# Splitting the first four operands of the second layer's y products during the last pair of h

## The chip, the cores and the metric

The kernel runs on one core of a Trainium2 chip. The metric is the device time in microseconds (us) of one execution; the times of several executions are compared by their median. The profiles are single executions recorded by the hardware profiler.

## What is computed

Chunked attention over 4 x 768 tokens feeds two feed-forward layers, each with an inner width of 2048 and an outer width of 512, in float32:

```python
def _moe_ref(x, w_in, w_out):
    h = x @ w_in
    g = h - np.tanh(h)
    return g @ w_out

def _moe2_ref(x, w_in, w_out, alpha):
    h = x @ w_in
    g = np.maximum(h, 0.0) + alpha * np.minimum(h, 0.0)
    return g @ w_out

def reference(...):
    attn_out = _attn_ref(**attn_kwargs)
    x = attn_out.transpose(0, 2, 1, 3).reshape(B * S, H * D)
    x = _moe_ref(x=x, **moe_kwargs)
    return _moe2_ref(x=x, **moe2_kwargs)
```

x has 3072 rows of 512, w_in is 512 x 2048 and w_out 2048 x 512.

## The kernel before

**Numbers in two parts.** Every float32 matrix that TensorE (PE) multiplies is split into a high part in fp32r and the rest (split_f32, and prep for the second layer's y): ScalarE (ACT) copies to fp32r, then VectorE (DVE) or GpSimd (POOL) subtracts. A product is three matmuls: high by high, high by rest, rest by high (PASS).

**Stages.** Attention and the first layer run together, in six blocks of 512 tokens (emit_h, emit_g, emit_y, evac_y). evac_y copies a finished block's four y tiles out of PSUM, two by ACT and two by DVE, and stores them to DRAM (y1d). In the sixth block the copies use a tag of their own, "zy" with two buffers. The second layer then runs in three blocks of 1024 tokens (the loop over b at L866). Each has an h stage and a y stage, and both save multiplications with Strassen's seven products (Winograd's variant) on 2 x 2 blocks.

**The h stage.** pair_h runs eight times in a block, for p = 0 to 7. It makes seven products of 6 matmuls (L404), in the source's order m = 1, 6, 5, 7, 2, 3, 4, and combines them in PSUM: hs is a copy of product 1 (ACT), hu adds product 6 (DVE), product 5 is added to hu (DVE, L421; called the d5 add here), hv is a copy of that (ACT, L446), and products 3 and 4 are accumulated on what the adds and copies leave. So product 3 waits for hv. prelu makes each of the four results of a pair: two ACT operations (L412, L413) and one DVE operation (L414), into gx or gy. Two POOL subtractions follow (L455 and L456).

**The y stage.** Its left operands are made from gx, gy and t3 by prep (L467 to L482), for s = 0 to 55, eight for each of the products in ORDER = (1, 6, 5, 2, 7, 3, 4). One prep is an ACT copy into go (L477) and a subtraction into go's second half (L479, the split), on DVE for most and on POOL for s = 2 to 7 and some later ones. For product 6 (s = 8 to 15) DVE first adds into a PSUM bank (L474) and afterwards updates gx (L481). y_product (L498) is 6 matmuls on one operand: the two with the high part first, or three for each of two banks. prep runs LEAD = 6 operands ahead in the source.

**What sets the order.** The Tile framework's scheduler orders each engine's instructions when the program is built. issue_after(ins) puts the instructions of a block that run on the engine of ins behind ins on that engine. On the chip each engine takes its instructions in that order. Tiles are given by pools; w has 34 buffers of 4 KB, which hold gx, gy, the operands of h and y, and half of the weights that load_in brings.

In the source all preps stand behind the last pair_h of a block:

```python
            for s in range(LEAD):
                prep(b, s)
            for s in range(7 * P2):
                if s + LEAD < 7 * P2:
                    prep(b, s + LEAD)
```

Of the kernel before, what the change touches and what calls it, by code (L numbers as in the profile page):

```python
# [7 lines left out]
FP32 = mybir.dt.float32  # L8
# [29 lines left out]
def chunk_attention_two_ffn_kernel(  # L38
# [12 lines left out]
    nc = tc.nc  # L51
# [10 lines left out]
    blocks1 = BLOCKS1  # L62
# [3 lines left out]
    def f32(ap):  # L66
        return ap.bitcast(FP32)

    const = ctx.enter_context(tc.tile_pool(name="const", bufs=1))
    w_p = ctx.enter_context(tc.tile_pool(name="w", bufs=2 * NF + 2))  # L70
# [17 lines left out]
    stage = {}  # L88
# [174 lines left out]
    last = {}  # L263
# [59 lines left out]

    def evac_y(l, b, n, t0):
        ys = yp.pop((l, b))
        for j, y in enumerate(ys):
            if l == 0 and b == len(blocks1) - 1:
                s = stage["z"].tile([128, 512], FP32, tag="zy", name="ys", bufs=2)
            else:
                s = t_p.tile([128, 512], FP32, tag="t", name="ys")  # L330
            dst = y1d[b, :, j, :] if l == 0 else out[(t0 + j) * 128:(t0 + j + 1) * 128, :]
            if j % 2 == 0:
                nc.scalar.activation(out=s, in_=y, func=ACTF.Copy)
            else:
                nc.vector.tensor_copy(out=s, in_=y)
            nc.scalar.dma_start(out=dst, in_=s)
# [5 lines left out]
    P2 = NF // 2  # L342
    NB = NTILE // 8
    NO = 7 * P2 // 2
    LEAD = 6
    wo2 = {}
    win = {}
    xop = {}
# [6 lines left out]
    def load_out(i):  # L355
        mi, pp = divmod(i % NO, P2 // 2)
        w = zr.tile([128, 2, 2, 256], FP32R, tag="wo", name="wo")
        nc.sync.dma_start(out=f32(w).rearrange("k p a n -> k (p a n)"), in_=w2o[ORDER[mi]][pp])
        wo2[i] = w

    def load_in(i, q):
        p = i % P2
        n = 2 if q < 3 else 1
        pool, tag = (w_p, "w") if i % 2 == 0 else (stage["z"], "z")
        w = pool.tile([128, 2, n, 256], FP32R, tag=tag, name="wi2")
        nc.sync.dma_start(
            out=f32(w).rearrange("p a s n -> p (a s n)"),
            in_=w2i[p][:, 1024 * q:1024 * q + 512 * n])
        win[i, q] = w
# [22 lines left out]
    def x2_work(b):  # L392
        return ([lambda w=w: load_x2(b, w) for w in (12, 11, 22, 21)]
                + [lambda m=m: sum_x2(b, m) for m in (5, 6, 7, 4)]
                + [lambda m=m: split_x2(b, m) for m in (1, 6, 5, 7, 2, 3, 4)])
# [14 lines left out]
    def prelu(t, h, f):  # L410
        n = t_p.tile([128, 512], FP32, tag="t", name="n")
        nc.scalar.activation(out=n, in_=h, func=ACTF.Relu, scale=-1.0)  # L412
        nc.scalar.activation(out=n, in_=n, func=ACTF.Copy, scale=alpha_neg[:, f:f + 1])  # L413
        nc.vector.scalar_tensor_tensor(  # L414
            out=t, in0=h, scalar=0.0, in1=n, op0=ALU.max, op1=ALU.add
        )

    def pair_h(i):
        b, p = divmod(i, P2)
# [40 lines left out]
    def y_bank(b, m):  # L460
        if (b % 2 == 0) == (m in (1, 6)):
            return ps_y.tile([128, 512], FP32, tag="y", name="yb")
        if m in (1, 5):
            return ps_h.tile([128, 512], FP32, tag="h", name="yb")
        return ps_h2.tile([128, 512], FP32, tag="h2", name="yb")

    def prep(b, s):  # L467
        mi, p = divmod(s, P2)
        m = ORDER[mi]
        x, y, d3 = gx[b, p], gy[b, p], t3[b, p // 2][:, p % 2]  # L470
        op = w_p.tile([128, 2, 512], FP32R, tag="w", name="go")
        if m == 6:
            src = y_bank(b, 7)
            nc.vector.tensor_tensor(out=src, in0=d3, in1=x[:, 0], op=ALU.add)  # L474
        else:
            src = {1: x[:, 0], 5: y[:, 0], 2: y[:, 1], 7: d3, 3: x[:, 1], 4: x[:, 0]}[m]
        nc.scalar.activation(out=op[:, 0], in_=src, func=ACTF.Copy)  # L477
        eng = nc.gpsimd if (m == 1 and p > 1) or (m not in (1, 6) and p % 4 == 3) else nc.vector
        eng.tensor_tensor(out=op[:, 1], in0=src, in1=f32(op[:, 0]), op=ALU.subtract)  # L479
        if m == 6:  # L480
            nc.vector.tensor_tensor(out=x[:, 0], in0=y[:, 1], in1=src, op=ALU.subtract)  # L481
        gop[b, s] = op  # L482
# [4 lines left out]
    def y_product(b, s, tiles=(0, 1)):  # L487
        mi, p = divmod(s, P2)
        m = ORDER[mi]
        into = {2: 1, 3: 5, 4: 7}.get(m, m)  # L490
        if m == into and p == 0 and 0 in tiles:
            yd[b, m] = [y_bank(b, m) for _ in range(2)]
        w = wo2[b * NO + mi * (P2 // 2) + p // 2][:, p % 2]
        w = w.rearrange("k a (i n) -> k a i n", i=2)
        op = gop[b, s]
        for i in tiles:
            for n, (a, c) in enumerate(PASS):
                nc.tensor.matmul(  # L498
                    out=yd[b, into][i], lhsT=w[:, a, i], rhs=op[:, c],
                    start=(m == into and p == 0 and n == 0), stop=(p == P2 - 1 and n == 2),  # L500
                    skip_group_check=True,
                )

    def y_done(b, m, tiles=(0, 1)):
        add = lambda o, p, q: nc.vector.tensor_tensor(out=o, in0=p, in1=q, op=ALU.add)
        if m in (1, 6, 5):
            for i in tiles:
                tag = "gl" if m == 6 else "gh"
                e = ye[b, m, i] = g_p.tile([128, 512], FP32, tag=tag, name="ye")
                d = yd[b, m][i]  # L510
                if m == 6:
                    add(e, d, ye[b, 1, i])
                    continue
                if m == 5:
                    add(d, d, ye[b, 6, i])
                nc.scalar.activation(out=e, in_=d, func=ACTF.Copy)
            return
        into, h, t = {2: (1, 0, 0), 7: (7, 1, 1), 3: (5, 0, 1), 4: (7, 1, 0)}[m]
        if 0 in tiles:
            ye[b, "st"] = w_p.tile([128, 16, 2, 32], FP32, tag="w", name="st")  # L520
        st = ye[b, "st"]
        for i in tiles:
            d = src = yd[b, into][i]
            if m == 7:
                src = t_p.tile([128, 512], FP32, tag="t", name="c")
                add(src, d, ye[b, 5, i])
                add(d, d, ye[b, 6, i])
            nc.vector.transpose(out=st[:, :, i], in_=src.rearrange("k (b n) -> k b n", n=32))
        t0 = 1024 * b + 512 * t
        split = len(tiles) == 1  # L530
        for a in range(4):
            dst = out[t0:t0 + 512, 256 * h + 64 * a:256 * h + 64 * a + 64]
            dst = dst.rearrange("(b i) (e j) -> i b e j", i=32, e=2)
            src = st[32 * a:32 * a + 32]
            if split:
                dst, src = dst[:, :, tiles[0]], src[:, :, tiles[0]]
            (nc.scalar if split and a % 2 else nc.sync).dma_start(out=dst, in_=src)
# [189 lines left out]
    if True:  # L727
# [138 lines left out]
        for b in range(NB):  # L866
            more = b + 1 < NB
            for p in range(P2):
                i = b * P2 + p
                if i > 0:  # L870
                    pair_h(i)
                for q in range(4):
                    win.pop((i, q))
                if p + 2 < P2:
                    for q in range(4):
                        load_in(i + 2, q)
            early, late = [], []
            if more:
                work = x2_work(b + 1)
                early, late = work[:8], work[8:]  # L880
                late[3:3] = [lambda q=q: load_in((b + 1) * P2, q) for q in range(4)]
                late += [lambda q=q: load_in((b + 1) * P2 + 1, q) for q in range(4)]
            for s in range(LEAD):
                prep(b, s)
            for s in range(7 * P2):
                if s + LEAD < 7 * P2:
                    prep(b, s + LEAD)
                if more or s < 6 * P2:
                    y_product(b, s)
                    if s % P2 == P2 - 1:  # L890
                        y_done(b, ORDER[s // P2])
                    i = b * NO + s // 2 + 4
                    if s % 2 and i < NB * NO:
                        load_out(i)
                if s >= 2 * P2 and s % 2 == 0 and early:
                    early.pop(0)()
                if s >= 4 * P2 and late:
                    late.pop(0)()
            if not more:
                for i in range(2):  # L900
                    for p in range(P2):
                        y_product(b, 6 * P2 + p, (i,))
                    y_done(b, 4, (i,))
# [61 lines left out]
```

## Time and profile before

| what | value |
| --- | --- |
| three runs | 1112.11, 1113.10, 1114.18 us; median 1113.1 |
| the profiled execution | 1113.69 us |
| its span, first to last instruction | 1111.9 us |
| PE busy | 1061.2 us, 95% of the span |
| DVE, ACT, POOL busy | 61%, 48%, 41% |
| mean granted TensorE clock | 0.986 of full speed |
| share of the chain that ended last | PE 88%, DVE 3%, DMA 3%, ACT 3%, issue 2%, POOL 1% |
| second layer | from about 616 us to the end |

A row of the timeline gives the start, the duration, the engine, the line, the operation with out<-in, how many instructions are merged, and in brackets the idle time of the engine just before with what ended it. PE matmuls are pipelined: one is drawn as about 0.39 us long, and the next begins 0.227 us after it.

### The profile page before, as it was taken

Reading aid. Unit: us, or ns where it says so; the run is one execution under the profiler, and the core shown is the slowest. Engines: PE = TensorE matmul, PEld = TensorE weight load, DVE = VectorE, ACT = ScalarE, POOL = GpSimd, SP = SyncE. Lnnn points to the kernel's source line nnn. Section 1 sums busy time; section 2 is a strip of 40 time slices with the busy share of each in tenths; the row PEclk is TensorE's granted clock in tenths of the full one; section 3 lists DMA queues with packets and bytes.
Section 4 is the critical chain, followed back from the end, with each engine's and each line's share of the span. In section 5 each row is a group of like instructions: output and inputs, shape, how many; then the busy total and the mean of one; then the engine's idle time right before and its main releaser. Section 6 shows DMA issues by size and latency. Waiting matters only on the chain.

```text
span 1111.9 us, 18216 instructions
## 1 busy us (share of the span) xinstructions
PE 1061.2 (95%) x6912; PEld 866.5 (78%) x6912; DVE 674.1 (61%) x1087; ACT 534.8 (48%) x956; POOL 459.5 (41%) x351
## 2 busy tenths in 40 slices
PE   5699999999999999999999999799998899998998
PEld 4488878888888888888888787688886688876786
DVE  3788765765755675565311355977455966456953
ACT  3566644453544454444332455654465644466540
POOL 3266634444544453444462122546122545122520
PEclk9899999999999999999999999899999899999999
DMA  9673144545564464464420644478835578642476
GB/s 277 259 266 114 58 161 143 199 125 200 182 204 171 145 214 154 156 217 146 134 67 1 220 159 170 147 245 275 242 137 185 166 233 280 209 169 97 152 211 168
DMA packets 99366, 196.22 MB, mean 176 GB/s; under 512 B 36560, under 2 KB 50896, under 8 KB 99280
## 3 DMA queue, kind: packets, MB, share of 16 engines
q1 hardware_dynamic: 93712, 188.52, 51.9%
q10 hardware_dynamic: 5568, 6.56, 1.6%
q8 instruction: 54, 0.88, 0.3%
q14 instruction: 32, 0.26, 0.1%
HBM read 153.10 MB, written 41.94 MB: 175 GB/s over the span
## 4 chain that ended last, share of the span: by engine, by line
PE 88%; DVE 3%; DMA 3%; ACT 3%; issue 2%; POOL 1%; SPq 0%; DVEq 0%; POOLq 0%; ACTq 0%
PE h L274 22%; PE y L313 22%; PE yb L498 20%; PE h L404 18%; PE pv L670 2%; PE sp L586 2%; DMA y1d<-ys 2%; DVE go L479 1%; ACT n L412 1%; DMA qn<-in_q_dram 1%; ACT n L413 1%; PE tp L657 1%; DMA ro<-in_moe_w_out_dram 1%; DVE yb L474 1%; DVE h L421 0%
## 5 line engine op out<-in xcount | busy, mean ns | idle before, releaser
L274 PE MATMUL h<-ring,wt 128*128 128x512 f32 x1152 | 282.2, 392 | 5.8 <-ACT ring L677 2.7
L274 PEld LDWEIGHTS h<-ring,wt 128*128 128x128 f32 x1152 | 216.7, 189 | 52.4 <-ACT ring L677 2.8
L498 PE MATMUL yb<-go,wo 128*128 128x512 f32 x1008 | 237.9, 398 | 16.9 <-DVE go L479 8.5
L498 PEld LDWEIGHTS yb<-go,wo 128*128 128x128 f32 x1008 | 192.6, 192 | 61.8 <-DVE go L479 12.3
L404 PE MATMUL h<-xh,wi 128*128 128x512 f32 x672 | 211.9, 392 | 3.2 <-ACT hs L439 1.2
L299 POOL TENSOR_TENSOR gl<-t,gh 128x512 fp32r<-128x512 f32 x96 | 129.6, 1352 | 173.8 <-ACT gh L298 158.0
L313 PE MATMUL y<-gh,wt 128*128 128x512 f32 x768 | 192.8, 391 | 0.0
L313 PEld LDWEIGHTS y<-gh,wt 128*128 128x128 f32 x768 | 143.1, 188 | 30.5
L290 DVE TENSOR_TENSOR t<-h,t 128x512 f32<-128x512 f32 x96 | 66.0, 687 | 144.6 <-ACT t L289 144.5
L404 PEld LDWEIGHTS h<-xh,wi 128*128 128x128 f32 x672 | 126.1, 188 | 35.1 <-ACT hv L446 5.4
L455 POOL TENSOR_TENSOR t<-gx,gy 128x512 f32<-128x512 f32 x24 | 31.1, 1296 | 200.6 <-DVE gy L414 200.6
L289 ACT ACTIVATE t<-h 128x512 f32<-128x512 f32 x96 | 56.9, 593 | 115.2 <-PE h L274 93.9
L313 PE MATMUL y<-gl,wt 128*128 128x512 f32 x384 | 104.3, 390 | 0.3 <-POOL gl L299 0.3
L298 ACT ACTIVATE gh<-t 128x512 fp32r<-128x512 f32 x96 | 60.5, 630 | 53.0 <-DVE t L290 51.4
L313 PEld LDWEIGHTS y<-gl,wt 128*128 128x128 f32 x384 | 71.9, 188 | 15.7 <-POOL gl L299 0.7
L404 PE MATMUL h<-xl,wi 128*128 128x512 f32 x192 | 74.7, 389 | 0.0
L122 POOL TENSOR_TENSOR ws<-sm,ws 128x512 fp32r<-128x512 f32 x32 | 42.6, 1333 | 57.8 <-ACT ws L121 42.2
L413 ACT ACTIVATE n<-n,alpha_neg 128x512 f32<-128x512 f32 x96 | 66.0, 719 | 0.4
L122 POOL TENSOR_TENSOR wt<-s,wt 128x512 fp32r<-128x512 f32 x32 | 41.3, 1294 | 39.8 <-ACT wt L121 38.1
L404 PE MATMUL h<-x,wi 128*128 128x512 f32 x144 | 56.0, 389 | 0.0
L477 ACT ACTIVATE go<-gx 128x512 fp32r<-128x512 f32 x72 | 41.0, 626 | 27.6 <-PE yb L498 15.9
L479 DVE TENSOR_TENSOR go<-gx,go 128x512 fp32r<-128x512 f32 x42 | 48.7, 1195 | 3.9 <-ACT go L477 3.9
(95 smaller groups left out, 1365.1 us busy)
## 6 DMA issues: line engine op xcount, KB each, us to landing
wo<-w2o SPq DMA_DIRECT2D x84, 512.0 KB, 4.4
wi<-w2i SPq DMA_DIRECT2D x72, 512.0 KB, 4.8
kn<-in_k_dram SPq DMA_DIRECT2D x24, 384.0 KB, 4.5
vn<-in_v_dram SPq DMA_DIRECT2D x24, 384.0 KB, 4.0
ri<-in_moe_w_in_dram SPq DMA_DIRECT2D x16, 512.0 KB, 7.6
ro<-in_moe_w_out_dram SPq DMA_DIRECT2D x16, 512.0 KB, 8.3
pk<-in_moe_w_in_dram SPq DMA_DIRECT2D x16, 512.0 KB, 4.0
pk<-in_moe_w_out_dram SPq DMA_DIRECT2D x16, 512.0 KB, 4.0
```

What stands on the lines that cost most here:

```text
L122: nc.gpsimd.tensor_tensor(out=lo, in0=v, in1=f32(hi), op=ALU.subtract)
L274: last["ffn"] = nc.tensor.matmul(out=h, lhsT=wi[:, a, kk, :], rhs=ring[c][:, s0:s0 + n, kk, :], start=(i == 0), stop=(i == 3 * KD - 1),).ins
L289: nc.scalar.activation(out=t, in_=h, func=ACTF.Tanh)
L290: last["dve"] = nc.vector.tensor_tensor(out=t, in0=h, in1=t, op=ALU.subtract).ins
L298: nc.scalar.activation(out=gh, in_=t, func=ACTF.Copy)
L299: nc.gpsimd.tensor_tensor(out=gl, in0=t, in1=f32(gh), op=ALU.subtract)
L313: mm = nc.tensor.matmul(out=yp[l, b][j][:, :n * 128], lhsT=wo[:, a, j * 128:(j + 1) * 128], rhs=g[c], start=first, stop=final,)
L404: nc.tensor.matmul(out=h, lhsT=w[:, a, 128 * kt:128 * kt + 128], rhs=x[c][:, kt, :], start=(first and j == 0), stop=(j == 5), skip_group_c ...
L413: nc.scalar.activation(out=n, in_=n, func=ACTF.Copy, scale=alpha_neg[:, f:f + 1])
L477: nc.scalar.activation(out=op[:, 0], in_=src, func=ACTF.Copy)
L479: eng.tensor_tensor(out=op[:, 1], in0=src, in1=f32(op[:, 0]), op=ALU.subtract)
L498: nc.tensor.matmul(out=yd[b, into][i], lhsT=w[:, a, i], rhs=op[:, c], start=(m == into and p == 0 and n == 0), stop=(p == P2 - 1 and n == ...
```

## The change

The first EARLY = 4 operands of a block's y stage are prepared ahead of the last pair_h in the source (prep itself is unchanged). The other preps are put behind last["pre"] with issue_after; that is the DVE instruction of the latest prelu, so only their DVE instructions are tied. evac_y's copies of the sixth block of the first layer use two tiles of pool w, each holding two of the four copies, in place of two buffers of tag zy.

```diff
     def evac_y(l, b, n, t0):
         ys = yp.pop((l, b))
+        final = l == 0 and b == len(blocks1) - 1
         for j, y in enumerate(ys):
-            if l == 0 and b == len(blocks1) - 1:
-                s = stage["z"].tile([128, 512], FP32, tag="zy", name="ys", bufs=2)
+            if final:
+                if j % 2 == 0:
+                    pair = w_p.tile([128, 2, 512], FP32, tag="w", name="ys")
+                s = pair[:, j % 2]
...
+    EARLY = 4
...
-        nc.vector.scalar_tensor_tensor(
+        last["pre"] = nc.vector.scalar_tensor_tensor(
             out=t, in0=h, scalar=0.0, in1=n, op0=ALU.max, op1=ALU.add
-        )
+        ).ins
...
             for p in range(P2):
                 i = b * P2 + p
+                if p == P2 - 1:
+                    for s in range(EARLY):
+                        prep(b, s)
                 if i > 0:
                     pair_h(i)
...
-            for s in range(LEAD):
-                prep(b, s)
+            with tc.issue_after(last["pre"]):
+                for s in range(EARLY, LEAD):
+                    prep(b, s)
             for s in range(7 * P2):
                 if s + LEAD < 7 * P2:
-                    prep(b, s + LEAD)
+                    with tc.issue_after(last["pre"]):
+                        prep(b, s + LEAD)
```

Line numbers of the changed kernel are four higher in pair_h and prep (L408 for L404, L425 for L421, L483 for L479, L502 for L498).

**PE at the first block's border between h and y.** The names are the scheduler's: h2 are the PSUM tiles of pair_h (the last pair has four numbers in a row; the third of them holds products 5 and 3, the fourth 7 and 4), yb those of y, go the split operands in the order of s. Before, the last product of h ends and y begins:

```order
L404 MATMUL h2_7021<-xh_6166,wi2_6938 128x512 x2
L404 MATMUL h2_7021<-xl_6167,wi2_6938 128x512
L404 MATMUL h2_7021<-xh_6166,wi2_6938 128x512
L498 MATMUL yb_7112<-go_7091,wo_6482 128x512
L498 MATMUL yb_7113<-go_7091,wo_6482 128x512
```

Now, from the end of product 5 of the last pair through its product 7:

```order
L408 MATMUL h2_7030<-xl_6089,wi2_6932 128x512
L408 MATMUL h2_7030<-xh_6088,wi2_6932 128x512
L502 MATMUL yb_7110<-go_7014,wo_6482 128x512
L502 MATMUL yb_7111<-go_7014,wo_6482 128x512
L408 MATMUL h2_7031<-xh_6092,wi2_6934 128x512
L408 MATMUL h2_7031<-xl_6093,wi2_6934 128x512
L408 MATMUL h2_7031<-xh_6092,wi2_6934 128x512 x2
L408 MATMUL h2_7031<-xl_6093,wi2_6934 128x512
L408 MATMUL h2_7031<-xh_6092,wi2_6934 128x512
L502 MATMUL yb_7110<-go_7014,wo_6482 128x512 x2
L502 MATMUL yb_7111<-go_7014,wo_6482 128x512 x2
L502 MATMUL yb_7110<-go_7017,wo_6482 128x512
```

The first y products stand between products of the last pair. The whole order from product 5 on is: 2 matmuls of s = 0, product 7, 4 of s = 0, 6 of s = 1, 2 of s = 2, product 3, 4 of s = 2, 2 of s = 3, product 4, 4 of s = 3, then s = 4 and on. It is the same at all three borders.

**DVE at the same border.** Before, from the d5 add of the last pair:

```order
L421 TENSOR_TENSOR h2_7020<-h2_7020,hu_7036 128x512
L421 TENSOR_TENSOR gx_7016<-h2_7021,hv_7045 128x512
L421 TENSOR_TENSOR h2_7021<-h2_7021,hu_7036 128x512
L414 SCALAR_TENSOR_TENSOR gx_7016<-gx_7016,n_7055 128x512
L414 SCALAR_TENSOR_TENSOR gx_7016<-h2_7018,n_7065 128x512
L414 SCALAR_TENSOR_TENSOR gy_7017<-h2_7020,n_7075 128x512
L414 SCALAR_TENSOR_TENSOR gy_7017<-h2_7021,n_7087 128x512
L474 TENSOR_TENSOR yb_7132<-t3_6408,gx_6406 128x512
L479 TENSOR_TENSOR go_7091<-gx_6406,go_7091 128x512
L474 TENSOR_TENSOR yb_7144<-t3_6408,gx_6523 128x512
L479 TENSOR_TENSOR go_7094<-gx_6523,go_7094 128x512
```

Now, from the last prelu of pair p = 6:

```order
L418 SCALAR_TENSOR_TENSOR gy_6939<-h2_6944,n_7010 128x512
L483 TENSOR_TENSOR go_7014<-gx_6406,go_7014 128x512
L425 TENSOR_TENSOR hu_7046<-h2_7029,hs_7038 128x512
L483 TENSOR_TENSOR go_7017<-gx_6521,go_7017 128x512
L425 TENSOR_TENSOR h2_7030<-h2_7030,hu_7046 128x512
L425 TENSOR_TENSOR gx_7026<-h2_7031,hv_7055 128x512
L425 TENSOR_TENSOR h2_7031<-h2_7031,hu_7046 128x512
L418 SCALAR_TENSOR_TENSOR gx_7026<-gx_7026,n_7065 128x512
L418 SCALAR_TENSOR_TENSOR gx_7026<-h2_7028,n_7075 128x512
L418 SCALAR_TENSOR_TENSOR gy_7027<-h2_7030,n_7085 128x512
L418 SCALAR_TENSOR_TENSOR gy_7027<-h2_7031,n_7097 128x512
L478 TENSOR_TENSOR yb_7130<-t3_6408,gx_6406 128x512
```

The splits of s = 0 and 1 moved from behind the last prelu to either side of hu. At the second border the first L474 also stood ahead of the d5 add before; now it is behind the last prelu there too.

**ACT at the same border.** Now, from the first pair of L413's of the last pair (n are the prelus' scratch tiles; the early four copies stand right ahead of hv and are not shown):

```order
L417 ACTIVATE n_7075<-n_7075,alpha_neg_79 128x512
L416 ACTIVATE n_7085<-h2_7030 128x512
L417 ACTIVATE n_7085<-n_7085,alpha_neg_79 128x512
L481 ACTIVATE go_7101<-gx_6771 128x512
L481 ACTIVATE go_7104<-gx_6855 128x512
L481 ACTIVATE go_7107<-gx_6938 128x512
L481 ACTIVATE go_7118<-gx_7026 128x512
L416 ACTIVATE n_7097<-h2_7031 128x512
L417 ACTIVATE n_7097<-n_7097,alpha_neg_79 128x512
L481 ACTIVATE go_7129<-yb_7130 128x512
```

Before, all eight copies (s = 0 to 7) stood behind the last prelu's L413. Four of them now stand ahead of hv, and four between the third and the last prelu of the pair. POOL now has, behind pair 6's L456: the splits of s = 2, 3 and 4, the last pair's L455, the splits of s = 5, 6 and 7, and the last pair's L456.

## Rows read from the trace of the kernel before

**Rows 1.** PE, groups by line from 640 us to the end: busy, mean ns, idle before.

```profile
L498 PE MATMUL yb<-go,wo 128*128 128x512 f32 x1008 | 237.9, 398 | 16.9 <-DVE go L479 8.5 <-ACT go L477 8.4
```

**Rows 2.** PE's timeline at the three borders between h and y.

```profile
695.91 0.40 PE L404 MATMUL h<-xh,wi 128*128 128x512 f32 x1
699.12 0.73 PE L498 MATMUL yb<-go,wo 128*128 128x512 f32 x2 [2.80 <-ACT go L477]
702.30 2.93 PE L498 MATMUL yb<-go,wo 128*128 128x512 f32 x6 [2.46 <-DVE go L479]
705.68 6.56 PE L498 MATMUL yb<-go,wo 128*128 128x512 f32 x23 [0.45 <-DVE go L479]
...
856.76 0.50 PE L404 MATMUL h<-xh,wi 128*128 128x512 f32 x1 [1.13 <-ACT hv L446]
...
859.41 0.40 PE L404 MATMUL h<-xh,wi 128*128 128x512 f32 x1
...
869.42 6.84 PE L498 MATMUL yb<-go,wo 128*128 128x512 f32 x24 [0.45 <-DVE go L479]
...
1022.81 0.40 PE L404 MATMUL h<-xh,wi 128*128 128x512 f32 x1
...
1032.57 7.77 PE L498 MATMUL yb<-go,wo 128*128 128x512 f32 x33 [0.45 <-DVE go L479]
```

**Rows 3.** The chain that ended last, y stage of the second block: start, length, matmuls.

```profile
930.21 19.04 PE yb L498 x84
```

**Rows 4.** Windows: us, busy (x) of PE, PEld, DVE, ACT, POOL, then granted clock, DMA.

```profile
628.40:629.50 1.10, 0.00 (x0) 0.00 (x0) 1.07 (x2) 1.08 (x2) 0.00 (x0) 1.00 0.24 93
705.20:707.00 1.80, 1.35 (x4) 1.14 (x4) 1.80 (x4) 0.00 (x0) 1.80 (x2) 0.50 0.00 0
1023.20:1026.00 2.80, 0.01 (x1) 0.00 (x0) 1.99 (x4) 2.80 (x6) 0.36 (x1) 0.90 0.00 0
```

**Rows 5.** ACT's timeline at the third border.

```profile
1015.18 1.33 ACT L413 ACTIVATE n<-n,alpha_neg 128x512 f32<-128x512 f32 x2
1019.50 0.60 ACT L446 ACTIVATE hv<-h 128x512 f32<-128x512 f32 x1 [2.99 <-DVE h L421]
...
1023.63 0.59 ACT L412 ACTIVATE n<-h 128x512 f32<-128x512 f32 x1
1024.11 1.33 ACT L413 ACTIVATE n<-n,alpha_neg 128x512 f32<-128x512 f32 x2
1025.34 4.26 ACT L477 ACTIVATE go<-gx 128x512 fp32r<-128x512 f32 x8
```

**Rows 6.** DVE's timeline: the third border, and three splits at 736.90 with POOL idle.

```profile
736.90 1.89 DVE L479 TENSOR_TENSOR go<-t,go 128x512 fp32r<-128x512 f32 x3
...
1015.93 1.30 DVE L414 SCALAR_TENSOR_TENSOR gy<-h,n 128x512 f32<-128x512 f32 x2 [0.99 <-ACT n L413]
1018.77 0.70 DVE L421 TENSOR_TENSOR h<-h,hu 128x512 f32<-128x512 f32 x1 [0.67 <-PE h L404]
...
1024.87 1.30 DVE L414 SCALAR_TENSOR_TENSOR gy<-h,n 128x512 f32<-128x512 f32 x2 [0.40 <-ACT n L413]
...
1027.39 1.75 DVE L479 TENSOR_TENSOR go<-gx,go 128x512 fp32r<-128x512 f32 x1
...
1032.44 0.68 DVE L479 TENSOR_TENSOR go<-yb,go 128x512 fp32r<-128x512 f32 x1
```

**Rows 7.** POOL's timeline: the third border, and a stretch of the first layer's sixth block.

```profile
562.93 4.77 POOL L122 TENSOR_TENSOR x<-x,xh 128x1024 fp32r<-128x1024 f32 x2
...
1016.70 1.30 POOL L455 TENSOR_TENSOR t<-gx,gy 128x512 f32<-128x512 f32 x1 [7.85 <-DVE gy L414]
1018.08 1.30 POOL L456 TENSOR_TENSOR gy<-gy,gx 128x512 f32<-128x512 f32 x1
```

**Rows 8.** Where the first layer's last y is copied out: ACT, then PE.

```profile
627.78 0.60 ACT L333 ACTIVATE ys<-y 128x512 f32<-128x512 f32 x1 [1.43 <-DMA y1d<-ys]
629.53 0.50 PE L404 MATMUL h<-xh,wi 128*128 128x512 f32 x1 [1.21 <-ACT hs L439]
```

## The prediction

> **What bounds the kernel now.** I read the shares of busy time first: PE is busy for 95% of the span, and the chain that ended last runs through PE for 88%. In the second layer PE therefore sets the time, and a change can win only where PE stands idle or runs slowly. The groups by line come next. From 640 us on, y's matmuls have 16.9 us of idle time ahead of them, all of it in waits for operands, half for ACT's copies and half for the splits [rows 1]. PE's timeline shows where: at each of the three borders between h and y there are three waits, at the first one 2.80, 2.46 and 0.45 us [rows 2].
>
> To price a border I need PE's undisturbed step. In the chain, 84 matmuls take 19.04 us, so 0.227 each [rows 3]. From the start of the last h matmul to the drawn end of the third group of y the borders take 16.33 us (695.91 to 712.24), 16.85 and 17.53, for 1+2+6+23 = 32, 33 and 42 matmuls [rows 2]. At 0.227 each, and 0.16 for the last one's drawn length, that should be 7.4, 7.65 and 9.7. The loss is 8.9, 9.2 and 7.8, together 25.9 us. Only 16.9 of it is idle time; the other 9.0, 3.0 per border, is matmuls at a slow clock: after the waits the window at 705.20 has a granted clock of 0.50, and that at 1023.20 an average of 0.90 [rows 4]. These are the full level of 2.4 GHz and the half of it.
>
> The cause of the waits is on ACT, DVE and POOL at the third border: the eight copies start at 1025.34, behind the last L413 [rows 5], and DVE's first split follows only after the last prelu and an L474 [rows 6].
>
> **The change: what PE gains.** Twenty-four matmuls, those of s = 0 to 3, can fill the border's idle time, and the first of them need nothing of the last pair. I walk through the third border with the times of before.
>
> ACT is done with pair 6 at 1015.18 + 1.33 = 1016.5 [rows 5]. Four copies at 4.26/8 = 0.53 end at 1018.6. That is ahead of hv (1019.50 before), so they cost ACT nothing. s = 0 and 1 are split on DVE, s = 2 and 3 on POOL. POOL is at work from 1016.70 without a break, in L455, L456 and then these splits [rows 7]. So DVE's splits run beside POOL, and I have to choose their price. A split alone takes 1.89/3 = 0.63; one beside POOL took 1.75 [rows 6]; waiting out a whole POOL operation would make it 1.30 + 0.63 = 1.93. I take 1.75, the row with the same operands and the same neighbour. An operation that reads PSUM, like hu and the d5 add, should stay near 0.6: the d5 add took 0.70 with L456 beside it [rows 6, 7].
>
> DVE is free at 1017.23. The split of s = 0 ends at 1019.0, hu (0.6 to the next operation) at 1019.6, the split of s = 1 at 1021.3, the d5 add at 1022.0 instead of 1019.47, and hv at 1022.6 instead of 1020.10. Product 3 waits for hv. But PE, which ends product 5 at about 1018.6 (the d5 add began at 1018.77 behind it), now has 20 matmuls before product 3, product 7 among them: 4.5 us, to 1023.1. So hv's 2.5 us are covered, with 0.5 to spare. Without the cover they would be the fourth wait of a border. Then come 18 matmuls, and product 4 ends at 1027.2 with 20 of the 24 early matmuls done.
>
> **What is left of the waits.** Four more operands (s = 4 to 7) and product 6's eight depend on the last pair still. ACT's copies of s = 4 to 7 begin where the last input of the last prelu stood, 4.0 us behind hv (1025.34 − 1020.10, less 0.59 and 0.66 for the L412 and L413 that now come later) [rows 5]. That is 1026.6, and s = 4 is split on POOL at 1028.5, just as PE wants it. L455 stands between (1.30), and s = 5 comes at 1031.1, while PE is there at 1029.9: a wait of 1.2.
>
> The rest hangs on DVE. The last prelu ended 6.07 us after hv; the four copies put between add 2.13, so it ends at 1022.6 + 8.2 = 1030.8. Everything of product 6 is queued behind it on DVE. Two L474 beside POOL's splits take 3.5 (to 1034.3), four more operations of 0.6 the first two operands (1036.7). Three pairs of operands at 6 x 0.6 = 3.6 follow, and without the last L481 the split of s = 15 is there at 1046.9, with 0.3 for three copies that DVE must wait for at 1047.2. Four matmuls are left then: 1048.1. PE without waits would need 4 + 72 matmuls from 1027.2, so 17.2 us, and end at 1044.4. So 3.7 us remain, wherever they fall. Some six restarts cost about 0.1 each (a matmul behind a wait is drawn 0.50 long, not 0.40 [rows 2]), which makes **4.2 us per border**.
>
> The bounds: if DVE's operations beside POOL took 0.6, hv and the last prelu would come 2.3 earlier and the two L474 2.3 sooner done, and nothing would be late, so 0; at 1.93 each the four of them add 0.7, so 5.0. If the clock fell as before, 3.0 more.
>
> **Other terms.** At the second border PE waited 1.13 for hv in the last pair [rows 2], since an L474 stood ahead of the d5 add there. It no longer does, so 1.1 is gained. Where the first layer's last y is copied out, ACT waits 1.43 for the DMA that stores an earlier tile, and PE then waits 1.21 for hs behind it [rows 8]. Two tiles of pool w for the four copies need no store to end: 1.2 gained. The copies themselves last as long. The tie costs no engine time. Later in y DVE keeps ahead of PE: six matmuls take 1.36 and a split alone 0.63, so tied operands are early enough. Against it stands the first layer's sixth block, where the scheduler's order changed without the source: POOL now has four splits of 4.77/2 = 2.4 us in a row [rows 7], 9.6 us, where at most two stood. I estimate 0.5 lost, between a gain of 1 and a loss of 2.
>
> **The sum.** 25.9 + 1.1 + 1.2 = 28.2 gained, less 3 x 4.2 = 12.6 and 0.5: 15.1 us. The profiled execution took 1113.69, span 1111.9; the median of the runs is 1113.1, 0.6 lower, and I set the forecast on the median: **1098.0 us**.
>
> **The rivals.** *A, the forecast* (60%): 1098, of its own between 1094 and 1102 by the unknown of the sixth block and 1 us per border.
>
> *B, the clock falls again* (16%). The 4.2 us left come as several waits close together. If PE then drops to half speed as it did before, each border pays its 3.0 again: 1101, 1104 or 1107 for one, two or three of them. For it: borders with 16.9/3 = 5.6 us of waits had the fall. Against it: a wait of 1.21 alone left the clock at 1.00 in the window at 628.40 [rows 4], and in the plan no single wait is longer. Beside this, the Trainium skill ("TensorE: Matmul & The Clock Gate", Part 1: The HAM clock gate) says that the clock is set by how busy the array has been recently, so that several small waits can count like a long one. By that rule the price is B's; the fall after the waits before agrees, and the 1.21 us wait neither proves nor denies it.
>
> *C, less contention* (16%). DVE's operations beside POOL cost nearer 0.6, and 0 to 2 us per border are left: 27.7 gained, or 6 less, so 1085 to 1091. For it: POOL's splits and DVE's need not overlap fully. Against it: the 1.75 of the row at 1027.39 [rows 6], the nearest there is.
>
> *D, the early splits hold up h* (4%). If hu, the d5 add and what stands behind are slowed beside POOL as well, product 3 waits for hv, and product 4 and the last prelu behind that. Each such operation costs 1.1 more, and there are seven to the last prelus. It decides from hv later than 1023.1; all seven are 7.7 us per border, less the spare 0.5: 21.6 for three, so about 1120. Against it: the d5 add's 0.70 beside L456 [rows 6, 7].
>
> *E, nothing comes of it* (4%): DVE is the limit through all of product 6 and more, and what PE gains in h it waits for there, 1111 to 1115.
>
> **How the numbers follow.** From A with its margin, most of C and nearly all of B: 1090 to 1106 holds about 8 in 10. About 0.2%, 2.2 us, is what a measurement of this kernel can tell from no change. A, B and C are faster by more than that: 0.92. E gives 0.04 for the same, D 0.04 for slower.
>
> **What would show it.** In the profile of the changed kernel: y's matmuls lie between the last products of h; the idle time ahead of y's matmuls in the second layer falls from 16.9 to about 11, in waits of at most 1.3 us, on POOL's split of s = 5 and DVE's L474; the granted clock stays at 1.00 at the borders; hv ends 2.5 us later with no wait of PE at product 3; the DMA wait of ACT and the wait for hs at 628 us are gone. Wrong would be: a wait ahead of product 3 (D), windows with 0.50 (B), DVE's early splits at 0.6 (C), or an idle time of y still at 16 (E).

## The result and the profile after

| | before | after |
| --- | --- | --- |
| median of four runs, us | 1113.3 | 1094.4 |
| lowest to highest | 1112.11 to 1114.18 | 1093.62 to 1096.97 |
| ratio (95% interval) | 1 | 0.9835 (0.9817 to 0.9854) |
| the profiled execution, its span | 1113.69, 1111.9 | 1096.97, 1094.1 |

The change is 18.9 us faster; 15.1 were forecast. The kernels were run on several chips, so the experiments below go by their ratio to the kernel before on the same chip. "Scaled" means that ratio times 1113.3.

The groups by line from 640 us to the end, PE of the kernel after (the first row answers to [rows 1]):

```profile
L502 PE MATMUL yb<-go,wo 128*128 128x512 f32 x1008 | 235.5, 392 | 5.8 <-DVE go L483 2.7 <-ACT go L481 1.8 <-POOL go L483 1.2
L408 PE MATMUL h<-xh,wi 128*128 128x512 f32 x610 | 192.5, 391 | 0.7 <-DVE gx L418 0.4
```

The idle time ahead of y's matmuls fell from 16.9 to 5.8 us, and no h matmul waits for hv or hs any longer. Where the rest is, PE's timeline of the kernel after shows, the second border first and then the third (answering to [rows 2]):

```profile
856.56 2.88 PE L502 MATMUL yb<-go,wo 128*128 128x512 f32 x12
859.84 4.59 PE L502 MATMUL yb<-go,wo 128*128 128x512 f32 x18 [0.40 <-POOL go L483]
866.08 6.16 PE L502 MATMUL yb<-go,wo 128*128 128x512 f32 x24 [1.65 <-DVE go L483]
873.27 32.10 PE L502 MATMUL yb<-go,wo 128*128 128x512 f32 x140 [1.04 <-DVE go L483]
...
1006.42 0.61 PE L502 MATMUL yb<-go,wo 128*128 128x512 f32 x2
...
1008.24 2.88 PE L502 MATMUL yb<-go,wo 128*128 128x512 f32 x12
1010.96 0.39 PE L408 MATMUL h<-xh,wi 128*128 128x512 f32 x1
...
1014.81 0.39 PE L408 MATMUL h<-xh,wi 128*128 128x512 f32 x1
1015.04 2.88 PE L502 MATMUL yb<-go,wo 128*128 128x512 f32 x12
...
1018.32 9.40 PE L502 MATMUL yb<-go,wo 128*128 128x512 f32 x40 [0.40 <-POOL go L483]
1027.95 3.31 PE L502 MATMUL yb<-go,wo 128*128 128x512 f32 x12 [0.23 <-ACT go L481]
1031.70 57.71 PE L502 MATMUL yb<-go,wo 128*128 128x512 f32 x252 [0.45 <-ACT go L481]
```

The early matmuls lie between the last products of h, and PE has no wait there. Behind h the first border (0.40, 0.23, 0.45 and 0.41 us) and the third have only small waits; the second has 1.65 and 1.04. By the prediction's own method the third border costs, from the last h matmul at 1014.81 to the end at 1089.41, 74.6 us for 317 matmuls, at 0.2267 each and 0.16 for the drawn end: 2.6 us. The first costs 3.2 and the second 4.5 in the same way, 10.3 together, where it was 25.9. Of the 10.3, the waits named here are 5.7; the rest are restarts and gaps too short to be drawn, all at the full clock.

The windows across the second and third border, with the granted clock as the third number from the end:

```profile
1012.00:1024.00 12.00, 11.60 (x52) 9.24 (x51) 8.64 (x12) 6.72 (x12) 8.46 (x6) 1.00 0.41 125
856.00:868.00 12.00, 9.95 (x42) 7.35 (x41) 9.37 (x11) 6.05 (x11) 8.87 (x6) 1.00 0.61 191
```

The clock stays at its full level, 2.4 GHz, where it had been at half [rows 4].

DVE, ACT and POOL of the kernel after at the third border, and in the last row DVE at the second:

```profile
1005.01 1.40 DVE L483 TENSOR_TENSOR go<-gx,go 128x512 fp32r<-128x512 f32 x1
...
1006.92 1.18 DVE L483 TENSOR_TENSOR go<-gx,go 128x512 fp32r<-128x512 f32 x1
1008.03 0.69 DVE L425 TENSOR_TENSOR h<-h,hu 128x512 f32<-128x512 f32 x1
...
1017.23 0.69 DVE L418 SCALAR_TENSOR_TENSOR gy<-h,n 128x512 f32<-128x512 f32 x1 [2.63 <-ACT n L417]
1017.84 2.68 DVE L478 TENSOR_TENSOR yb<-t,gx 128x512 f32<-128x512 f32 x2
...
1008.75 0.60 ACT L450 ACTIVATE hv<-h 128x512 f32<-128x512 f32 x1 [2.30 <-DVE h L425]
...
1005.93 1.63 POOL L460 TENSOR_TENSOR gy<-gy,gx 128x512 f32<-128x512 f32 x1
...
859.35 6.08 DVE L478 TENSOR_TENSOR yb<-t,gx 128x512 f32<-128x512 f32 x4
```

The early splits took 1.40 and 1.18 us. hv ends at 1009.35 and product 3 begins at 1010.96, so hv has 1.6 us to spare (two of the expectations below reckon with 1.4). DVE then stands idle for 2.63 us ahead of the last prelu, with product 6's work tied behind it. At the second border four L478 in a row stand between the last prelu and the first split of product 6.

### The profile page after: what moved, and what is told of

The parts are those of the page before. It is cut to its first block, busy times and chain, and to the rows that moved or that the text cites. A ratio compares the mean times of both kernels' runs of the same rounds, so it can differ in the third digit from the quotient of the medians.

```text
span 1094.1 us, 18216 instructions
## 1 busy us (share of the span) xinstructions
PE 1056.4 (97%) x6912; PEld 863.4 (79%) x6912; DVE 677.7 (62%) x1087; ACT 535.2 (49%) x956; POOL 464.3 (42%) x351
## 5 line engine op out<-in xcount | busy, mean ns | idle before, releaser
L502 PE MATMUL yb<-go,wo 128*128 128x512 f32 x1008 | 235.5, 392 | 5.8 <-DVE go L483 2.7
L502 PEld LDWEIGHTS yb<-go,wo 128*128 128x128 f32 x1008 | 187.9, 188 | 51.1 <-DVE go L483 5.3
L408 PE MATMUL h<-xh,wi 128*128 128x512 f32 x672 | 212.1, 391 | 0.7 <-DVE gx L418 0.4
L299 POOL TENSOR_TENSOR gl<-t,gh 128x512 fp32r<-128x512 f32 x96 | 127.0, 1325 | 173.3 <-ACT gh L298 150.6
L408 PEld LDWEIGHTS h<-xh,wi 128*128 128x128 f32 x672 | 126.2, 188 | 30.6 <-ACT hv L450 2.9
L459 POOL TENSOR_TENSOR t<-gx,gy 128x512 f32<-128x512 f32 x24 | 31.1, 1295 | 175.1 <-DVE gy L418 175.1
L408 PE MATMUL h<-xl,wi 128*128 128x512 f32 x192 | 74.8, 390 | 0.0
L483 DVE TENSOR_TENSOR go<-gx,go 128x512 fp32r<-128x512 f32 x42 | 57.3, 1406 | 1.4 <-ACT go L481 1.4
L408 PE MATMUL h<-x,wi 128*128 128x512 f32 x144 | 56.1, 390 | 0.0
L483 POOL TENSOR_TENSOR go<-gx,go 128x512 fp32r<-128x512 f32 x30 | 44.0, 1479 | 20.0 <-ACT go L481 20.0
```

The lines of the kernel that those rows point to most:

```text
L299: nc.gpsimd.tensor_tensor(out=gl, in0=t, in1=f32(gh), op=ALU.subtract)
L408: nc.tensor.matmul(out=h, lhsT=w[:, a, 128 * kt:128 * kt + 128], rhs=x[c][:, kt, :], start=(first and j == 0), stop=(j == 5), skip_group_c ...
L459: nc.gpsimd.tensor_tensor(out=d3, in0=gb[1], in1=ga[1], op=ALU.subtract)
L502: nc.tensor.matmul(out=yd[b, into][i], lhsT=w[:, a, i], rhs=op[:, c], start=(m == into and p == 0 and n == 0), stop=(p == P2 - 1 and n == ...
```

## The experiments: the parts one by one

**The new evac_y alone.** The source is that of the change with

```diff
-    EARLY = 4
+    EARLY = 0
...
-            with tc.issue_after(last["pre"]):
-                for s in range(EARLY, LEAD):
-                    prep(b, s)
+            for s in range(EARLY, LEAD):
+                prep(b, s)
...
-                    with tc.issue_after(last["pre"]):
-                        prep(b, s + LEAD)
+                    prep(b, s + LEAD)
```

> The kernel before with the new evac_y alone (two tiles of pool w instead of two buffers of tag zy). Theory (PE's wait of 1.21 us for hs behind the store goes, and nothing takes its place): 1.2 us faster, some 1112.1, no DMA wait of ACT at the copies of the last y, the borders as before (16.9 us idle ahead of y). Rival (the wait is slack that comes back at the next product, or the two tiles of pool w delay a load): 1113.3, no change.

Measured: 1112.0, ratio 0.9989 (0.9976 to 1.0001), scaled 1.2 us faster. PE's wait for hs is gone, and so is the 0.27 us for POOL's gl in the first layer's sixth block. The size is as expected; the interval just takes in no change.

**The new evac_y and the tie.** EARLY = 0, the tie as in the change.

> The change without its early operands (EARLY = 0): new evac_y and the tie. Theory (the early operands bring nearly everything): 1.2 from evac_y and 1.1 from the wait for hv at the second border, some 1111.0; the three borders keep their 16.9 us of idle time and the granted clock of 0.50 behind it. Rival (the tie is what helps, because DVE has its preludes' work first and the last prelu comes earlier at every border): 1104 or less, idle ahead of y under 12 us.

Measured: 1113.3, ratio 1.0000 (0.9990 to 1.0010). Both expectations fall. PE's timeline of this run at the second border:

```profile
859.44 1.22 PE L502 MATMUL yb<-go,wo 128*128 128x512 f32 x2 [2.79 <-ACT go L481]
865.97 2.93 PE L502 MATMUL yb<-go,wo 128*128 128x512 f32 x6 [5.31 <-DVE go L483]
```

The wait for hv is gone there, but the second wait grew from 2.75 to 5.31 us. DVE now does three L478 (4.75 us, from 859.51) between the last prelu and the first split. Before, one stood there, and two had gone ahead of the last prelu, as the kernel before shows (PE's second wait, then DVE):

```profile
866.05 2.93 PE L498 MATMUL yb<-go,wo 128*128 128x512 f32 x6 [2.75 <-DVE go L479]
...
853.75 1.73 DVE L474 TENSOR_TENSOR yb<-t,gx 128x512 f32<-128x512 f32 x1
...
861.12 0.70 DVE L474 TENSOR_TENSOR yb<-t,gx 128x512 f32<-128x512 f32 x1
```

So in the trace the tie alone costs 2.6 us and gives 1.1 back. In time this run is 1.3 us slower than the one before it, on the same chip; the two intervals overlap, so the time alone would not show it.

**No tie.** The change with the two issue_after blocks taken out, EARLY = 4.

> The change without the tie. DVE then does one or two L478 ahead of the last prelu: at the second border right behind the d5 add, at the others in the wait for ACT between the third and the last prelu. Theory (hv is done before that L478 and has spare time anyway): within 1 us of the change, 1093.5 to 1095.5, and less idle time ahead of product 6 at the first and third border. Rival (the tie is needed: each L478 beside POOL costs 1.75 us that the last prelu and all behind it come later): 1097 to 1100.

Measured: 1091.7, ratio 0.9806 (0.9791 to 0.9822), scaled 3.2 us faster than the change (the two intervals just meet). The rival is wrong in direction, and the theory said too little, and for the wrong place: at the third border PE's waits are about as in the change (0.28, 0.47 and 0.48 us). The gain is at the second border. DVE there, then PE:

```profile
848.60 1.19 DVE L478 TENSOR_TENSOR yb<-t,gx 128x512 f32<-128x512 f32 x1
...
853.58 0.70 DVE L478 TENSOR_TENSOR yb<-t,gx 128x512 f32<-128x512 f32 x1
...
878.96 1.38 PE L502 MATMUL yb<-go,wo 128*128 128x512 f32 x5 [1.10 <-DMA wo<-w2o]
```

Two L478 are done early, ahead of the two last prelus, and the waits of 1.65 and 1.04 are gone. A wait for a weight load of 1.10 us has come instead.

**evac_y as before.** The change with the old tag zy, two buffers, in evac_y.

> The change with evac_y as before. Theory (the three parts add up): 1.2 us slower than the change, 1095.6, with PE's wait for hs of 1.2 us back at about 628 us. Rival (evac_y's part is worth nothing): 1094.4.

Measured: 1097.4, ratio 0.9857 (0.9840 to 0.9874), scaled 2.4 us slower than the change. PE's timeline of this run shows more than the one wait (lines here are two lower):

```profile
548.09 1.20 PE L313 MATMUL y<-gl,wt 128*128 128x512 f32 x4 [0.36 <-POOL gl L299]
631.87 0.50 PE L406 MATMUL h<-xh,wi 128*128 128x512 f32 x1 [0.96 <-ACT hs L441]
659.00 0.47 PE L406 MATMUL h<-xh,wi 128*128 128x512 f32 x1 [0.60 <-DMA wi<-w2i]
```

0.36 + 0.96 + 0.60 = 1.9 us, without the restarts. The traces show what evac_y's part does: the waits for gl and for hs are gone with the new copies and back with the old. What that is worth in time is not shown, since the intervals of this run and the change overlap, and that of the new evac_y alone takes in no change.

**The tie behind the third prelu.** The change with

```diff
-        prelu(gb[0], d[7], f + 1)
+        keep = last["pre"]; prelu(gb[0], d[7], f + 1); last["pre"] = keep
```

> The change with the tie behind the third prelu of the last pair in place of the fourth. DVE then has one L478 (and the first operand's split) ahead of the last prelu at the first and third border, three L478 at the second. Theory (what the tie costs, 2.7 us against the run without it, is DVE standing idle 2.6 us per border for ACT ahead of the last prelu, with product 6's work queued behind it): most of it comes back, 1091.7 to 1093. Rival (the tie costs in the rest of y, where every later DVE operand is tied too): 1094.4, as the change.

Measured: 1096.1, ratio 0.9836 (0.9821 to 0.9851): as the change. The theory's time is missed. DVE and PE of this run at the second border, and a window across the last of these rows:

```profile
854.39 5.19 DVE L478 TENSOR_TENSOR yb<-t,gx 128x512 f32<-128x512 f32 x3
...
860.23 20.01 PE L502 MATMUL yb<-go,wo 128*128 128x512 f32 x87 [1.98 <-DVE go L483]
885.12 29.09 PE L502 MATMUL yb<-go,wo 128*128 128x512 f32 x120 [2.38 <-DMA wo<-w2o]
...
870.00:890.00 20.00, 17.62 (x71) 14.09 (x70) 18.59 (x23) 12.27 (x23) 7.25 (x5) 0.91 0.77 279
```

At the first and third border DVE has product 6's work earlier, and PE's waits are about as in the change (0.28, 0.46 and 0.44 at the third). The second border still has L478 in a row, three in 5.19 us, and 1.98 us of wait, with a load's wait of 2.38 behind it. Behind that single wait the clock fell: 0.09 of the 20 us window is missing, 1.8 us of full clock. The run without any tie waits 1.10 us for a load and keeps its clock, so some 3 us of the profiled execution come from the load. Without them the run would be near 1093, the upper end of the theory: it decides for neither expectation.

**The tie in the first and third block only.** The second block's preps are tied to an earlier prelu, the last of pair 6:

```diff
+            tie = last["pre"] if b != 1 else last["early"]
...
-            with tc.issue_after(last["pre"]):
+            with tc.issue_after(tie):
```

> The change with the tie in the first and third block only; the second block's later operands are free to go ahead of its last prelus (there DVE then has one L478 behind the d5 add and one between the prelus, not four in a row behind the last prelu). Theory (the tie costs its 2.7 us at the second border alone, where four L478 stand ahead of the first operand of product 6 and PE waits 1.65 and 1.04 us): 1091.7 to 1092.5, ratio to the kernel before about 0.981, and no wait of DVE's making over 0.6 us at the second border. Rival (the cost lies at all borders or in the rest of y): 1093.5 to 1094.4.

Measured: 1091.5, ratio 0.9794 (0.9776 to 0.9812), as without any tie, and below the change's interval. The only wait left at the second border is 1.50 us for a load of wo. So the tie's cost sits at the second border, and the order of DVE there is its cause: shown by undoing it in that block alone. (The later operands of that block are free as well; that it is the border that counts is read from PE's waits of 1.65 and 1.04, which are gone.)

## The experiments: how many early operands

These three have the new evac_y and no tie, and EARLY = 1, 2, 3. The runs with none and four are above.

> New evac_y, no tie, one early operand (with none 1112.0, with four 1091.7: 20.3 us, 6.8 per border). Theory (of the 6.8, 3.0 are the clock's fall, which goes in one step as soon as the waits at a border are short enough; the other 3.8 come evenly, 0.95 per operand): the clock still falls, so 1109.2. Rival (no step, 1.7 per operand and border): 1106.9.

> As before with two early operands. Theory (step): 1106.3 with the granted clock at 0.50 behind the waits at all three borders, or 1097.3 with 1.00 at all three, or 3 us between for each border; nothing else. Rival (even): 1101.9 whatever the clock.

> As before with three early operands. Theory (step): 1094.5, granted clock 1.00 at the borders (1103.5 if it still fell at all). Rival (even): 1096.8.

| early operands | median, us | ratio (interval) | scaled gain | idle ahead of y, us |
| --- | --- | --- | --- | --- |
| 0 | 1112.0 | 0.9989 (0.9976 to 1.0001) | 1.2 | 17.3 |
| 1 | 1106.6 | 0.9929 (0.9914 to 0.9944) | 7.9 | 13.9 |
| 2 | 1103.4 | 0.9903 (0.9888 to 0.9918) | 10.8 | 12.1 |
| 3 | 1093.0 | 0.9816 (0.9800 to 0.9832) | 20.5 | 5.3 |
| 4 | 1091.7 | 0.9806 (0.9791 to 0.9822) | 21.6 | 3.8 |

Scaled times are 1105.4, 1102.5 and 1092.8 us for one, two and three. The theory said 1109.2, 1106.3 (with the clock at half at all three borders, as it was) and 1094.5; the rival said 1106.9, 1101.9 and 1096.8.

Windows of 12 us across the third border, with none, one, two and three early operands in this order:

```profile
1018.00:1030.00 12.00, 6.30 (x15) 3.95 (x14) 11.19 (x12) 7.85 (x15) 9.11 (x6) 0.73 0.00 0
1018.00:1030.00 12.00, 7.61 (x24) 5.47 (x23) 10.98 (x12) 7.38 (x14) 9.73 (x7) 0.72 0.15 44
1018.00:1030.00 12.00, 8.61 (x30) 6.27 (x29) 9.74 (x13) 7.30 (x14) 9.76 (x7) 0.86 0.25 80
1009.00:1021.00 12.00, 10.85 (x46) 7.97 (x45) 10.10 (x13) 6.02 (x12) 10.13 (x7) 1.00 0.29 93
```

PE's waits there, with two early operands (first two rows) and with three:

```profile
1020.49 0.73 PE L502 MATMUL yb<-go,wo 128*128 128x512 f32 x2 [1.36 <-ACT go L481]
1023.25 6.93 PE L502 MATMUL yb<-go,wo 128*128 128x512 f32 x22 [2.03 <-POOL go L483]
...
1011.53 2.42 PE L502 MATMUL yb<-go,wo 128*128 128x512 f32 x8 [0.61 <-POOL go L483]
1014.48 6.87 PE L502 MATMUL yb<-go,wo 128*128 128x512 f32 x29 [0.52 <-POOL go L483]
```

From two to three the gain jumps by 9.7 us. Of that 6.8 is idle time (12.1 to 5.3). The other 2.9 are put down to the clock, which fell to 1.2 GHz behind waits of 1.36 and 2.03 us and stayed at 2.4 GHz with 0.61 and 0.52; what of the slow stretch falls into a wait costs nothing more. The single matmuls of the trace bear that out: with two early operands 20 more of them than with three take some 0.43 us to the next, in place of 0.227. So there is a step, but idle time is more than two thirds of it, and my numbers for it were wrong in two ways. The idle time did not fall evenly: with two early operands POOL splits s = 2 and 3 late, and PE waits 6.2 us for POOL in all, against 2.9 with three. (Waits for loads of wo make no difference between them, 1.8 and 1.7 us.) And the fall is not all or nothing: with two early operands 0.14 of the 12 us is missing, 1.7 us of full clock, and with one 0.28, so 3.4. The time with two, scaled 1102.5, is close to the even rival's 1101.9, and only the windows and the run with three tell them apart.

## The experiments: what hv's lateness costs

**The early splits twice.** In prep, behind the split:

```diff
+        if s < 2: eng.tensor_tensor(out=op[:, 1], in0=src, in1=f32(op[:, 0]), op=ALU.subtract)
```

> The change with the early splits of s = 0 and 1 done twice on DVE (the second writes the same values), so that the d5 add, hv and everything behind them come 1.2 to 2.5 us later at each border. Theory (hv has 1.4 us to spare at product 3, but what is behind it, the copies of s = 4 to 7, the last prelu and product 6, passes its lateness on to PE almost whole): 1.0 to 2.5 us per border, 1097.5 to 1102. Rival (the last prelu's lateness is slack as well): 1094.4.

Measured: 1104.9, ratio 0.9912 (0.9893 to 0.9931), scaled 8.6 us slower than the change, 2.9 per border, over both expectations. PE's first wait at the third border of this run (lines behind the addition are one higher):

```profile
1015.21 4.71 PE L503 MATMUL yb<-go,wo 128*128 128x512 f32 x18 [1.44 <-DVE go L484]
```

Half of the loss is PE waiting for the second write of s = 0, which the experiment itself put there. It does not answer its question, so a cleaner one followed.

**Two more DVE subtractions into a scratch tile.** The added line writes to a tile that nobody reads:

```diff
+        if s < 2: nc.vector.tensor_tensor(out=t_p.tile([128, 512], FP32, tag="t", name="n"), in0=src, in1=f32(op[:, 0]), op=ALU.subtract)
```

> The change with two more DVE subtractions in the last pair of each block, like the early splits but into a scratch tile that nobody reads: one ahead of hu, one ahead of the d5 add. So no operand waits for its second split, as in the run before; only hu, the d5 add and hv are later, by some 2.8 us (1.2 to 1.75 each beside POOL). Theory (hv has 1.4 us to spare at product 3, what goes over is a wait there, and the rest of the lateness reaches PE by way of the copies of s = 4 to 7 and the last prelu): 2.3 to 2.8 us per border in all, 1101.5 to 1103. Rival (behind product 3 there is slack, so that only the 1.4 us over the spare time cost): 1098.6 or less.

Measured: 1103.8, ratio 0.9908 (0.9888 to 0.9927), scaled 8.1 us slower than the change, 2.7 per border. ACT, then PE of this run at the third border:

```profile
1018.09 0.60 ACT L450 ACTIVATE hv<-h 128x512 f32<-128x512 f32 x1 [5.70 <-DVE h L425]
...
1023.60 0.73 PE L503 MATMUL yb<-go,wo 128*128 128x512 f32 x2 [0.94 <-ACT go L481]
1024.96 1.66 PE L503 MATMUL yb<-go,wo 128*128 128x512 f32 x6 [0.62 <-POOL go L483]
1027.44 9.36 PE L503 MATMUL yb<-go,wo 128*128 128x512 f32 x40 [0.82 <-POOL go L483]
```

hv ended 7.7 us after the first early split began; in the change it was 4.3, so it is 3.4 later. PE does not sit idle at product 3, because the scheduler put six more y matmuls ahead of it, but it waits for the copies of s = 4 to 7 and their splits. The theory's size holds, not its wait at product 3: some four fifths of hv's lateness (2.7 of 3.4) reach PE, by way of what is queued behind it.

**All early splits on POOL, no tie.** The reverse: DVE does no early split. The change without the tie and with

```diff
-        eng = nc.gpsimd if (m == 1 and p > 1) or (m not in (1, 6) and p % 4 == 3) else nc.vector
+        eng = nc.gpsimd if m == 1 or (m not in (1, 6) and p % 4 == 3) else nc.vector
```

> The change without the tie and with the splits of s = 0 and 1 on POOL, ahead of L460, so that DVE has none of the early splits. Theory (what is left of the borders is set by the time of hv): hv comes about 1.3 us earlier, and with it product 6; against that PE waits up to 0.6 us for POOL's split of s = 0. Between 1088.5 and 1091.7, the kernel without the tie. Rival (POOL's chain of four splits becomes the bound, 1.3 us each against 1.36 of PE, and s = 4 and 5 come late): 1093 or more.

Measured: 1089.05, ratio 0.9768 (0.9751 to 0.9784), scaled 2.9 us faster than the kernel with the tie in two blocks (0.9794, on the same chip) and 4.2 faster than the one without it (0.9806). POOL at the third border, then PE's y group from 640 us on:

```profile
999.71 2.54 POOL L483 TENSOR_TENSOR go<-gx,go 128x512 fp32r<-128x512 f32 x2
1002.20 1.29 POOL L460 TENSOR_TENSOR gy<-gy,gx 128x512 f32<-128x512 f32 x1
1003.45 2.56 POOL L483 TENSOR_TENSOR go<-gx,go 128x512 fp32r<-128x512 f32 x2
...
L502 PE MATMUL yb<-go,wo 128*128 128x512 f32 x1008 | 233.0, 390 | 1.8 <-ACT go L481 1.5 <-DMA wo<-w2o 0.3
```

With DVE out of the way POOL's splits take 1.27 us each, PE does not wait for them, and 1.8 us of idle time are left in all of y. hv ends 1.5 us behind product 5 (1001.84 against the next matmul at 1000.31), 1.4 earlier than in the change; 1.3 were expected. The time, scaled to 1087.5, is 1.0 below the expected range. Of the 2.0 us of idle time that went against the run without the tie, 1.1 were waits for loads, so how much of the 4.2 us is hv's is not shown. This version beats both kernels.

## Why the prediction was right, and where it was off

The mechanism held at each step but one: y's matmuls cover the borders, hv comes later without a wait at product 3, the clock stays up, the wait for hs and the store goes; only the tie did not come free. The time, 1094.4, lies within the range and 3.6 below the forecast. By its own terms:

- **The borders.** Forecast 4.2 us left on each, 12.6 together; measured 3.2, 4.5 and 2.6, together 10.3. Idle time ahead of y was to fall to about 11 in waits of at most 1.3; it fell to 5.8, with one of 1.65. The sum hides two errors of opposite sign, the price beside POOL and the tie. Without the tie the kernel runs at 1091.7, so that the forecast came as near as it did is in part luck.
- **The slow clock.** I put all of the 9.0 us that were not idle time down to it, 3.0 per border. That was too much. Six matmuls that stand as 2.93 in [rows 2] are drawn as 1.52 at the full clock; by such comparisons I estimate that 6.5 of the 9.0 are the clock and the rest restarts behind waits. The kernel after has such a loss without any fall: the 4.6 us of restarts and short gaps at a clock of 1.00. The total lost, 25.9, does not change by this, but rival B's price does.
- **The price beside POOL.** I took 1.75 us, the one row at hand [rows 6], for every operation. The early splits took 1.40 and 1.18, two L478 2.68 together: an operation pays for what is left of the POOL operation that it meets (last section), and only one that meets it near its start pays 1.75. POOL's pays too (L460 1.63, alone 1.30). So hv comes 2.9 us behind product 5 (1009.35 against the next matmul at 1006.42), not 4.0. The wait of 1.2 us for s = 5 came as 0.40. The experiments with hv later or earlier show that this was the right chain to follow: its lateness goes through to PE.
- **The last prelu.** Forecast 8.2 us behind hv, measured 8.6 (1017.23 + 0.69 − 1009.35).
- **The tie.** "The tie costs no engine time" and "1.1 is gained" for hv at the second border. The 1.1 was gained, but the order there, which I took to be that of the other borders, has four L478 in a row, 6.08 us. The waits of 1.65 and 1.04 come of them, and the tie costs about 3 us on balance, where the sum had it as a gain of 1.1. That is the step that failed.
- **evac_y.** Forecast 1.2; 1.2 alone, and 2.4 when taken out of the change, with waits for gl and for a load beside the one for hs. Neither time is clear of the scatter; that the wait goes is.
- **The sixth block.** Forecast 0.5 lost. PE's wait of 0.27 us for gl went away instead.

25.9 − 10.3 + 1.1 + 1.2 + 0.3 = 18.2 of the 18.9 measured. The rest is less than the runs scatter.

Of the rivals, B (the clock falls again) did not come about at four early operands, but it is what happens at two, at about 1 us per border (2.9 for three) and not 3.0. The waits of 1.36 and 2.03 us there are together 3.4, where the borders before had 5.2 to 6.0, and the clock fell all the same; 1.65 and 1.04 with some 6 us of matmuls between them left it at 1.00. A single wait of 2.38 (the tie behind the third prelu) brought the clock down, while 0.94, 0.62 and 0.82, also 2.38 together (two more DVE subtractions), left it at 1.00. The sum of idle time decides nothing by itself: ahead of y it was 12.2 in that run and 12.1 with two early operands. That agrees with the rule of the Trainium skill ("TensorE: Matmul & The Clock Gate", Part 1: The HAM clock gate) that it is how busy the array has lately been that sets the clock. C (less contention) was half true, D and E are excluded by the rows.

## What to carry to other kernels

At a border between stages look for operands of the next stage that need nothing of the last step, and let their matmuls fill the wait; a wait cut short enough also keeps the clock up, and that came here in a step, between two operands and three. Read the order of every engine at every border before costing a tie: one border with another order took back 3 us. And put the extra vector work on the engine that is not in the chain which releases the next product.

## What was not expected of the hardware

A DVE operation that reads two SBUF tiles had no fixed price beside POOL: 1.18, 1.40 and 1.75 us were seen where a split alone takes 0.63, and POOL's own operation grew from 1.30 to 1.63. Yet it follows a pattern that I had overlooked. POOL before, beside the 1.75 of [rows 6], and after, beside the first early split:

```profile
1027.00 1.60 POOL L456 TENSOR_TENSOR gy<-gy,gx 128x512 f32<-128x512 f32 x1
...
1004.56 1.29 POOL L459 TENSOR_TENSOR t<-gx,gy 128x512 f32<-128x512 f32 x1 [7.84 <-DVE gy L418]
```

The 1.75 ends at 1029.14, 0.54 us behind L456's end; the 1.40 at 1006.41, 0.56 behind L459's; the 1.18 at 1008.10, 0.54 behind L460's. In the run without the tie all 54 such operations that began while a POOL operation ran ended 0.55 to 0.56 us behind it. So there the price is what is left of POOL's operation plus about 0.55. It can fall on POOL instead: in the change, 51 of 55 follow the pattern, and the other four pass a POOL split that began at 888.08 and took 7.43 us, while DVE's own ran at 0.68 each. With both engines at work without a break it is 1.70 each: ACT's copies behind the four L478 of the second border start at 860.37, 862.08, 863.77 and 865.47. An operation with an input in PSUM, like hu and the d5 add, kept its 0.69.

The low clock had no fixed cost either: 12 us averaged 0.72 after the longer waits and 0.86 after the shorter ones. And as y came earlier, waits for loads of wo appeared: 1.10, 1.50 and 2.38 us at 879 to 885 us in three of the runs, 1.81 and 1.68 at 728 to 731 in the runs with two and three early operands. Why they come there and not in the change was not tried.
